# Attention into an expert layer on one core: short score transposes first, an ACT copy in each slot's chain, softmax work on DVE behind that chain

## The chip, the core and the metric

The kernel runs on one core of one Trainium2 chip. The core has a matrix engine (TensorE, PE in the profile; its weight loads are the row PEld), a vector engine (VectorE, DVE), an activation engine (ScalarE, ACT), GpSimd (POOL) and SyncE (SP), which here only issues DMAs. The metric is the device time of one execution in microseconds, as the median of several runs.

## What is computed

Memory attention for 8 batches and 8 heads, 576 positions of 64 numbers, with 32 memory slots, followed by one expert layer (a SiLU between two matrix products) over all 4608 tokens of 512 numbers, with 2048 hidden units. All in float32.

```python
a = softmax(phi, axis=2)                       # phi: 8 x 8 x 576 x 32
k_m = einsum('bhsm,bhsd->bhmd', a, k)          # 32 memory keys a head
v_m = einsum('bhsm,bhsd->bhmd', a, v)
attn = softmax(q @ k_m.T / 8, axis=-1)         # 576 x 32 a head
x = attn @ v_m                                 # to 4608 x 512
h = x @ w_in
out = (h * sigmoid(h)) @ w_out
```

## The kernel before

The product attn @ v_m @ w_in is folded: for each batch, v_m times w_in gives a small matrix `pm` (256 rows for 8 heads of 32 slots, `p_mm`), and the hidden values are `pm` times the attention weights. Each float32 factor is split into a high part, rounded to a shorter format (fp32r), and a low part, the rest; a product is high x high + high x low + low x high. A high part is a copy that rounds, a low part a subtraction.

The eight batches run one after another. Batches 0 and 1 use plain products, batches 2 to 7 a Strassen form of the second product (7 products of sums in place of 8). A batch of the second kind has 16 slots (2 halves t of the tokens, 8 steps j each). In one slot:

- PE computes the hidden values of the slot (`ffn1s`, L807, 12 matmuls into the PSUM tile `h`, of which there is one), then the matmuls of events, then the second product of the slot before (`st_step`, through `product` at L838, 21 matmuls: 14 with high parts, tile `aparts`, then 7 with low parts, tile `gparts`).
- `forms` turns `h` into the factors of the second product: ACT applies SiLU (L818, into `gbuf`; L820 does the leftover tokens, into `gleft`, and with it `h` is read) and rounds three of the blocks (L822). DVE forms four differences (L823, L826, L827), and rounds and subtracts. This is called the slot's chain here.
- Events put the attention of the next batch between the slots. By slot, in batches 2 to 6: 1, 2 and 3 are phi's maximum, its fold over partitions and its subtraction on DVE (L256 to L313); 4 its exponential on ACT (L317); 5 and 7 the products with k and v (`e_mm`, L333); 8 their transposes (`e_tr`, and the copy L366); 9 the scores (`s_all`), which go into PSUM as 512 columns a pair in the tile `bg` and 64 columns a pair in a free part of `h`, and are transposed by DVE from both; 10 the scores' maximum and subtraction on DVE (L424, L428); 11 their exponential on ACT (L432); 12, 13 sum and scaling (L436, L442); 14 transposes back (L453) and the split of the weights (`s_high` L458, `s_low` L463). `p_mm` in slots 1, 3, 13 and 15 is followed by its own split (ACT L644, DVE L646).
- After slots 7 and 15 `st_out` adds up the sums and stores them (ACT L869, seven DVE additions at L874).

What orders the work: PE's instructions stay in the order of the code throughout, ACT's from batch 1 on. DVE's order there is found by the scheduler at build time, within the dependencies; `behind(i, other)` adds a dependency of order between two instructions. ACT's functions lie in tables, so an exponential between SiLUs comes with two table loads (ACT_TABLE_LOAD).

Of the kernel before, what the change touches and what calls it, by code (L numbers as in the profile page):

```python
# [15 lines left out]
AF = mybir.ActivationFunctionType  # L16
ALU = mybir.AluOpType
# [10 lines left out]
JW = 512  # L28
# [20 lines left out]
def attn_ffn_kernel(  # L49
# [9 lines left out]
    nc = tc.nc  # L59
# [60 lines left out]
    raws, cvas, last_silu, last_split = {}, {}, [], []  # L120
# [249 lines left out]
    def s_all(b):  # L370

        sc = at[b]["sc"] = sb.tile([P, 2, S], F32, tag="att", name=f"sc{b}")
        bg, left = bgtile(), beside_h(S - 512)
        kvT = at[b]["kvT"]
        w = 512 - HALF
        for hf, f, n in ((0, 0, HALF), (1, 0, w), (1, w, HALF - w)):
            for r in range(NR):
                for p in range(2):
                    to = left[p] if f else bg[:, p, hf * HALF : hf * HALF + n]
                    nc.tensor.matmul(  # L380
                        to[M * r : M * (r + 1)],
                        kvT[D * p : D * (p + 1), 0, r],
                        at[b]["q", hf][D * p : D * (p + 1), r, f : f + n],
                        start=True, stop=True, skip_group_check=True,
                    )
        for p in range(2):
            nc.vector.transpose(sc[:, p, :512], bg[:, p])
        for p in range(2):
            nc.vector.transpose(sc[:, p, 512:], left[p])  # L389

    def s_mm(b, hf):
        if "sc" not in at[b]:
# [208 lines left out]
    ALL, FIRST, SECOND = (0, S), (0, HALF), (HALF, S)  # L601
# [211 lines left out]
    def forms(b, t, j, h):  # L813


        g = form_src
        w = MAIN // 2
        nc.scalar.activation(gbuf[:, :MAIN].rearrange("p (i f) -> p i f", i=2), h[:, :, :w], AF.Silu)  # L818
        o = b % 2 * LEFT + t * (LEFT // 2)
        nc.scalar.activation(gleft[:, 2 * j : 2 * j + 2, o : o + LEFT // 2], h[:, :, w:HALF], AF.Silu)  # L820
        hi, lo = form_high[j % 2], form_low[j % 2]
        nc.scalar.activation(hi[:, :3], g[:, 1:4], AF.Copy)  # L822
        nc.vector.tensor_tensor(  # L823
            g[:, 4:6], g[:, :1].broadcast_to([P, 2, P]), g[:, 1:3], op=ALU.subtract
        )
        nc.vector.tensor_tensor(g[:, 6], g[:, 1], g[:, 5], op=ALU.subtract)  # L826
        nc.vector.tensor_tensor(g[:, 7], g[:, 3], g[:, 6], op=ALU.subtract)  # L827
        nc.vector.tensor_copy(hi[:, 3:], g[:, 4:])  # L828
        nc.vector.tensor_tensor(lo, g[:, 1:], hi, op=ALU.subtract)  # L829
        return hi, lo  # L830

    def product(bank, place, part, k, w, first):
# [86 lines left out]
    events = {}  # L919

    def ev(b, slot, fn, *a):
        events.setdefault((b, slot), []).append((fn, a))

    for b in range(B):
        n = b + 1
        if b == 0:
            for j in range(2, DFF // CW):
                ev(b, 2 * j - 1.5, p_mm, b, j * CW, CW)
        elif b == 1:
            ev(b, 0, win_save)  # L930
            for j in range(1, NJ):
                ev(b, 4 * j - 3, p_mm, b, j * JW, JW)
            for j in range(NP):
                ev(b, 1.5 * j + 2, w_forms, j, 0)
                ev(b, 1.5 * j + 2.5, w_forms, j, 1)
        else:
            ev(b, 0, win_load, b, 3)
            ev(b, 1, p_mm, b, 2 * JW, JW)
            ev(b, 3, p_mm, b, 3 * JW, JW)
            if b > 2:  # L940
                ev(b, 1, s_high, b, SECOND)
                ev(b, 1, s_low, b, SECOND)
        if n == B:
            continue
        at_slot = (
            (4, 5, 6, 7.5, 9, 9.5, 11.5, 12.5, 13, 13.5, 13.5, 14) if b == 0
            else (1, 2, 3, 5, 9, 10, 10, 11, 12, 13, 13, 14) if b == 1
            else (1, 2, 4, 5, 8, 9, 9, 10, 11, 12, 13, 14)
        )
        mx, sub, ex, em, tr, s0, s1, sx, se, ss, sn, sk = at_slot  # L950
        ev(b, mx, phi_max, n)
        if n == 1:
            ev(b, sub, phi_allmax, n, (0, 1), (0,))
            ev(b, sub + 0.5, phi_allmax, n, (0, 1), (1,))
        else:
            for i in range(3):
                ev(b, sub, phi_fold, n, i)
        ev(b, 3 if b > 1 else sub + 0.5, phi_sub, n)
        ev(b, ex, phi_exp, n)
        if n < 3:  # L960
            ev(b, em, e_mm, n)
            ev(b, 14 if b == 0 else em + 1, load_kv, n + 1, range(FULLC if b == 0 else 2))
        else:
            ev(b, em, e_mm, n, range(2))
            ev(b, em, load_kv, n, range(2, FULLC))
            ev(b, em + 2, e_mm, n, range(2, FULLC))
            if n + 1 < B:
                ev(b, em + 2, load_kv, n + 1, range(2))
        ev(b, tr, e_tr, n)
        ev(b, em, load_q, n, 1)  # L970
        if n == 1:
            ev(b, s0, s_mm, n, 0)
            ev(b, s1, s_mm, n, 1)
        else:
            ev(b, s0, s_all, n)
        if n + 1 < B:
            ev(b, s1, load_q, n + 1, 0)
        ev(b, sx, s_max, n, ALL)
        ev(b, sx, s_sub, n, ALL)
        ev(b, se, s_exp, n, ALL)  # L980
        ev(b, ss, s_sum, n, ALL)
        ev(b, sn, s_norm, n, ALL)
        u = ALL if n < 3 else FIRST
        ev(b, sk, s_back, n, u)
        ev(b, sk, s_low, n, u)
        if n + 1 < B:
            ev(b, sk, load_phi, n + 1)
        if b == 0:
            ev(b, 14, p_mm, n, 0, JW)
        else:  # L990
            for k in range(3):
                ev(b, 6 + k if b == 1 and k < 2 else 10 + 2 * k, win_load, n, k)
            for k in range(2):
                ev(b, (12 if b == 1 else 13) + 2 * k, p_mm, n, k * JW, JW)
# [115 lines left out]
    def behind(i, other):  # L1110
        tc.add_manual_dep(
            i,
            other.ins.name,
            mybir.DependencyInfo(mybir.DependencyClass.NoSync, mybir.DependencyReason.DATA),
            reason="behind",
        )

    def finish(tiles):
        if prev is None:
            return  # L1120
        if prev[0] == "main":
            main_step(prev[1], prev[2], prev[3], tiles)
        elif prev[0] == "left" and tiles[0] == 0:
            if prev[1] < 2:
                left_step(prev[1], prev[2], prev[3])
                t1_load(prev[2])
            else:
                left_st(prev[1], prev[2], prev[3])
        elif prev[0] == "st" and tiles[0] == 0:
            st_step(*prev[1:])  # L1130

    for b in range(B):
        if b == 1:
            whole.close()
            ctx.enter_context(in_order(ACT))
        for s in range(NFC if b > 1 else 0):
            t, j = divmod(s, NP)
            h = ffn1s(b, t, j)
            part = forms(b, t, j, h)
            for part_ in range(2):  # L1140
                for fn, a in events.pop((b, s + part_ / 2), []):
                    fn(*a)
            finish(range(NI))
            prev = ("st", b, t, j, part)
        for fc in range(NFC if b < 2 else 0):
            if b == 0 and fc < 2:
                for part in range(2):
                    for fn, a in events.pop((b, fc + part / 2), []):
                        fn(*a)
                continue  # L1150
            h = ffn1(b, fc)
            gs = split(silu(b, fc, h))
            for part in range(2):
                if b == 0:
                    finish((2 * part, 2 * part + 1))
                traced = nc.cur_bb.bb.instructions
                n = len(traced)
                for fn, a in events.pop((b, fc + part / 2), []):
                    fn(*a)
                if b == 0:  # L1160
                    for i in list(nc.cur_bb.bb.instructions)[n:]:
                        if i.engine == ACT:
                            behind(i, last_silu[-1])
                        elif i.engine == DVE and fc > 10:
                            behind(i, last_split[-1])
            if b:
                finish(range(NI))
            prev = ("main", b, fc, gs)
        if b % 2:
            for n in range(NLS):  # L1170
                gs = left_split(b, n)
                finish((0, 1, 2, 3))
                prev = ("left", b, n, gs)
# [56 lines left out]
```

## Time and profile before

| | us |
|---|---|
| median of 3 runs | 711.97 (710.71 to 712.09) |
| the profiled execution | 712.11 |
| its span | 710.2 |
| PE busy in the span | 682.6 (96%) |
| PE's weight loads busy | 601.2 (85%) |
| DVE busy | 549.4 (77%) |
| ACT busy | 307.6 (43%) |

Busy shares are means over stages with different limits; batches 2 to 7 fill the span from 200.9 us on. A row of the order of time has the start in us from the span's start, the duration in us, engine, line, operation, result<-sources, shape and count, and in brackets the idle time of that engine just before and what ended it. A row of a group has busy time in us, mean duration in ns, then idle time before. A row of waits has who waited for whom: us in total, times, the longest. A row of a stretch has, for each engine, busy us, and then the share of the clock granted to PE.

### The profile page before, as it was taken

What the parts mean: (1) busy time and instruction counts of PE and PEld (TensorE: products, weight loads), DVE (VectorE), ACT (ScalarE), POOL (GpSimd) and SP (SyncE); (2) the same over time, 40 slices, a digit from 0 to 9 for tenths busy, and PEclk for the clock granted to TensorE, in tenths of its full rate; (3) what the DMA queues carried; (4) which work ended last, traced back from release to release, by engine and by line L of the source; (5) the groups of instructions that cost most, each with busy time, mean ns of one, the idle gap of its engine ahead of it and who ended that gap; (6) DMA issues with size and microseconds to landing.
All of it is one profiled execution on the core that took longest, in us unless ns stands there. A gap on an engine that the chain in (4) does not pass through costs nothing.

```text
span 710.2 us, 14595 instructions
## 1 busy us (share of the span) xinstructions
PE 682.6 (96%) x5932; PEld 601.2 (85%) x5932; DVE 549.4 (77%) x1109; ACT 307.6 (43%) x578; POOL 0.7 (0%) x6
## 2 busy tenths in 40 slices
PE   8999999999999989998999989999899998999997
PEld 3578777887889988898988989889889998889996
DVE  4898799788776778968869687887886867886663
ACT  3879674534524344342513424453432433442320
POOL 0000000000000000000000000000000000000000
PEclk9999999999999999999999999999999999999999
DMA  9998966304441344034420254203541024300001
GB/s 344 336 349 254 338 234 220 107 36 156 160 140 59 118 176 152 32 112 179 154 90 16 76 216 152 90 18 122 212 153 45 2 60 149 116 35 1 31 1 45
DMA packets 32946, 93.88 MB, mean 132 GB/s; under 512 B 2928, under 2 KB 13296, under 8 KB 29296
## 3 DMA queue, kind: packets, MB, share of 16 engines
q1 hardware_dynamic: 31936, 90.19, 36.3%
q10 hardware_dynamic: 944, 2.77, 1.0%
q8 instruction: 47, 0.77, 0.4%
q14 instruction: 19, 0.16, 0.1%
HBM read 77.22 MB, written 15.73 MB: 131 GB/s over the span
## 4 chain that ended last, share of the span: by engine, by line
PE 55%; DVE 22%; ACT 5%; issue 3%; DVEq 0%; ACTq 0%
PE sum L838 20%; PE h L807 15%; PE acc L706 6%; PE lsum L838 5%; DVE gparts L829 4%; PE h L665 4%; PE bg L628 2%; DVE oo L874 2%; DVE pm L646 2%; ACT gbuf L818 2%; DVE gbuf L823 2%; PE accleft L706 2%; PE bg L333 1%; DVE aparts L828 1%; DVE aT L453 1%
## 5 line engine op out<-in xcount | busy, mean ns | idle before, releaser
L807 PE MATMUL h<-aparts,pm 128*128 128x288 f32 x1152 | 170.9, 298 | 10.0 <-DVE sc L389 10.0
L818 ACT ACTIVATE gbuf<-h 128x512 f32<-128x512 f32 x96 | 57.4, 598 | 273.2 <-PE h L807 191.3
L807 PEld LDWEIGHTS h<-aparts,pm 128*128 128x128 f32 x1152 | 158.7, 190 | 11.0 <-issue 10.8
L829 DVE TENSOR_TENSOR gparts<-gbuf,aparts 128x896 fp32r<-128x896 f32 x96 | 104.7, 1091 | 8.4
L838 PE MATMUL sum<-wo_hi,aparts 128*128 128x256 f32 x384 | 105.6, 297 | 0.0
L838 PE MATMUL sum<-kept,aparts 128*128 128x256 f32 x576 | 101.2, 284 | 1.5 <-DVE oo L874 1.3
L838 PE MATMUL sum<-wo_lo,aparts 128*128 128x256 f32 x384 | 101.4, 285 | 0.0
L823 DVE TENSOR_TENSOR gbuf<-gbuf 128x256 f32<-128x256 f32 x96 | 40.7, 424 | 78.3 <-ACT gbuf L818 78.0
L838 PEld LDWEIGHTS sum<-wo_hi,aparts 128*128 128x128 f32 x384 | 74.2, 193 | 20.9 <-issue 12.7
L706 PE MATMUL acc<-wo_hi,gparts 128*128 128x512 f32 x256 | 86.4, 396 | 0.2
L838 PEld LDWEIGHTS sum<-kept,aparts 128*128 128x128 f32 x576 | 83.5, 193 | 2.3 <-DVE oo L874 2.3
L838 PEld LDWEIGHTS sum<-wo_lo,aparts 128*128 128x128 f32 x384 | 74.5, 194 | 0.0
L838 PE MATMUL sum<-wo_hi,gparts 128*128 128x256 f32 x384 | 73.8, 284 | 0.5
L838 PE MATMUL sum<-kept,gparts 128*128 128x256 f32 x288 | 65.5, 282 | 0.0
L838 PEld LDWEIGHTS sum<-wo_hi,gparts 128*128 128x128 f32 x384 | 59.3, 190 | 1.8 <-DVE gparts L829 1.5
L706 PEld LDWEIGHTS acc<-wo_hi,gparts 128*128 128x128 f32 x256 | 47.8, 188 | 14.2 <-DVE gparts L682 2.0
L665 PEld LDWEIGHTS h<-aparts,pm 128*128 128x128 f32 x372 | 51.7, 188 | 8.6 <-issue 2.3
L665 PE MATMUL h<-aparts,pm 128*128 128x288 f32 x372 | 56.3, 299 | 1.9 <-DVE aparts L463 1.0
L706 PE MATMUL acc<-wo_lo,gparts 128*128 128x512 f32 x128 | 50.5, 394 | 0.8 <-DVE wo_lo L182 0.8
L822 ACT ACTIVATE aparts<-gbuf 128x384 fp32r<-128x384 f32 x96 | 50.4, 525 | 0.0
L838 PEld LDWEIGHTS sum<-kept,gparts 128*128 128x128 f32 x288 | 47.9, 190 | 0.0
L828 DVE CAST aparts<-gbuf 128x512 fp32r<-128x512 f32 x96 | 40.7, 424 | 8.1 <-DVE phi L313 0.3
(197 smaller groups left out, 927.7 us busy)
## 6 DMA issues: line engine op xcount, KB each, us to landing
win<-win_saved SPq DMA_DIRECT2D x24, 1024.0 KB, 4.8
kv<-in_kv SPq DMA_DIRECT2D x28, 516.0 KB, 4.6
q<-in_q SPq DMA_DIRECT2D x16, 576.0 KB, 6.6
raw<-in_w_in SPq DMA_DIRECT2D x14, 512.0 KB, 7.8
out<-oo SPq DMA_DIRECT2D x27, 256.0 KB, 2.2
raw<-in_w_out SPq DMA_DIRECT2D x6, 1024.0 KB, 6.0
win_saved<-win SPq DMA_DIRECT2D x4, 1024.0 KB, 8.7
phi<-in_phi SPq DMA_DIRECT2D x7, 576.0 KB, 5.6
```

Source lines behind the costliest of these rows:

```text
L628: nc.tensor.matmul(bg[M * r : M * (r + 1), p, :w].rearrange("p (k f) -> p k f", f=P), kvT[D * p : D * (p + 1), 1, r], src[D * p : D * (p + ...
L646: nc.vector.tensor_tensor(lo[:, :, c], bg[:, :, :w], hi[:, :, c], op=ALU.subtract)
L665: nc.tensor.matmul(h[:, hf, :HALF], wt[:, p, fs], a[:, p, hf * HALF : (hf + 1) * HALF], start=n[hf] == 0, stop=n[hf] == 5, skip_group_chec ...
L706: nc.tensor.matmul(acc[key], gt[:, cs], wt[:, fc], start=fc == 0 and n == 0, stop=fc == NFC - 1 and n == 2)
L807: nc.tensor.matmul(h[:, i, :HALF], wt[:, p, f : f + P], a[:, p], start=n == 0, stop=n == 5)
L818: nc.scalar.activation(gbuf[:, :MAIN].rearrange("p (i f) -> p i f", i=2), h[:, :, :w], AF.Silu)
L822: nc.scalar.activation(hi[:, :3], g[:, 1:4], AF.Copy)
L823: nc.vector.tensor_tensor(g[:, 4:6], g[:, :1].broadcast_to([P, 2, P]), g[:, 1:3], op=ALU.subtract)
L828: nc.vector.tensor_copy(hi[:, 3:], g[:, 4:])
L829: nc.vector.tensor_tensor(lo, g[:, 1:], hi, op=ALU.subtract)
L838: nc.tensor.matmul(sums[bank][:, place * Q : (place + 1) * Q], gt[:, k], wt, start=bank not in begun, stop=True, skip_group_check=True,)
L874: nc.vector.tensor_tensor(to, a, c, op=op)
```

## The change

Four edits. In `s_all` the transposes of the two 64-column pieces (in `h`) come ahead of those of the 512-column pieces (in `bg`). In `forms` the rounding of the four differences moves from DVE to ACT (L828 after), and the one subtraction of seven blocks becomes two, of three (L829 after) and of four blocks (L830 after). In the batches from 2 on, every DVE instruction that an event issues, but those of `s_all`, is put behind the last subtraction of its slot's chain. And two events move: the split of the second half of the tokens from slot 1 to slot 6, and `p_mm` of slot 3 to the second half of that slot.

```diff
         for p in range(2):
+            nc.vector.transpose(sc[:, p, 512:], left[p])
+        for p in range(2):
             nc.vector.transpose(sc[:, p, :512], bg[:, p])
-        for p in range(2):
-            nc.vector.transpose(sc[:, p, 512:], left[p])
...
-        nc.vector.tensor_tensor(g[:, 7], g[:, 3], g[:, 6], op=ALU.subtract)
-        nc.vector.tensor_copy(hi[:, 3:], g[:, 4:])
-        nc.vector.tensor_tensor(lo, g[:, 1:], hi, op=ALU.subtract)
+        s4 = nc.vector.tensor_tensor(g[:, 7], g[:, 3], g[:, 6], op=ALU.subtract)
+        nc.scalar.activation(hi[:, 3:], g[:, 4:], AF.Copy)
+        behind(nc.vector.tensor_tensor(lo[:, :3], g[:, 1:4], hi[:, :3], op=ALU.subtract).ins, s4)
+        last_split.append(nc.vector.tensor_tensor(lo[:, 3:], g[:, 4:], hi[:, 3:], op=ALU.subtract))
...
-            ev(b, 3, p_mm, b, 3 * JW, JW)
+            ev(b, 3.5, p_mm, b, 3 * JW, JW)
             if b > 2:
-                ev(b, 1, s_high, b, SECOND)
-                ev(b, 1, s_low, b, SECOND)
+                ev(b, 6, s_high, b, SECOND)
+                ev(b, 6, s_low, b, SECOND)
...
                 for fn, a in events.pop((b, s + half_slot / 2), []):
+                    traced = nc.cur_bb.bb.instructions
+                    n = len(traced)
                     fn(*a)
+                    for i in list(nc.cur_bb.bb.instructions)[n:]:
+                        if i.engine == DVE and fn is not s_all:
+                            behind(i, last_split[-1])
```

Where instructions stand now. First DVE in batch 2 at the scores' transposes, from the end of slot 8's additions to the end of slot 9's chain (`sc` are the scores, `x` and `oo` the additions), before:

```order
L874 TENSOR_TENSOR oo<-x,sum_2121 128x256
L823 TENSOR_TENSOR gbuf<-gbuf 128x256
L826 TENSOR_TENSOR gbuf<-gbuf 128x128
L387 STREAM_TRANSPOSE sc_2573<-bg 128x512
L827 TENSOR_TENSOR gbuf<-gbuf 128x128
L387 STREAM_TRANSPOSE sc_2573<-bg 128x512
L828 CAST aparts<-gbuf 128x512
L389 STREAM_TRANSPOSE sc_2573<-h 128x64
L829 TENSOR_TENSOR gparts<-gbuf,aparts 128x896
L389 STREAM_TRANSPOSE sc_2573<-h 128x64
```

and after:

```order
L823 TENSOR_TENSOR gbuf<-gbuf 128x256
L875 TENSOR_TENSOR oo<-x,oo 128x256
L826 TENSOR_TENSOR gbuf<-gbuf 128x128
L875 TENSOR_TENSOR oo<-oo 128x256
L875 TENSOR_TENSOR oo<-x,oo 128x256
L875 TENSOR_TENSOR oo<-x,sum_2123 128x256
L827 TENSOR_TENSOR gbuf<-gbuf 128x128
L829 TENSOR_TENSOR gparts<-gbuf,aparts 128x384
L387 STREAM_TRANSPOSE sc_2583<-h 128x64 x2
L830 TENSOR_TENSOR gparts<-gbuf,aparts 128x512
L389 STREAM_TRANSPOSE sc_2583<-bg 128x512 x2
```

Both readers of `h` stand ahead of the long transposes now, and behind the first low part of the chain, whose first pieces stand among the additions.

Second ACT in batch 2 at phi's exponential, slot 4, before:

```order
L818 ACTIVATE gbuf<-h 128x512
L820 ACTIVATE gleft<-h 128x2x32
L822 ACTIVATE aparts<-gbuf 128x384
L317 ACT_TABLE_LOAD
L317 ACTIVATE phi_1900<-phi_1900 128x1152
L818 ACT_TABLE_LOAD
```

and after:

```order
L818 ACTIVATE gbuf<-h 128x512
L820 ACTIVATE gleft<-h 128x2x32
L822 ACTIVATE aparts<-gbuf 128x384
L828 ACTIVATE aparts<-gbuf 128x512
L317 ACT_TABLE_LOAD
L317 ACTIVATE phi_1900<-phi_1900 128x1152
L818 ACT_TABLE_LOAD
```

The exponential stands behind the new copy; so does the scores' (L432) in slot 11. On DVE the work that leads to it, before (phi's subtraction, then slot 0's chain, the first of the batch):

```order
L310 TENSOR_TENSOR phi_1900<-phi_1900,am 128x512
L313 TENSOR_TENSOR phi_1900<-phi_1900,am 64x128
L310 TENSOR_TENSOR phi_1900<-phi_1900,am 128x512
L313 TENSOR_TENSOR phi_1900<-phi_1900,am 64x128
L823 TENSOR_TENSOR gbuf<-gbuf 128x256
```

and after (the end of slot 3's chain, phi's subtraction, the low part of `pm`, and slot 4's chain):

```order
L830 TENSOR_TENSOR gparts<-gbuf,aparts 128x512
L310 TENSOR_TENSOR phi_1900<-phi_1900,am 128x512
L313 TENSOR_TENSOR phi_1900<-phi_1900,am 64x128
L310 TENSOR_TENSOR phi_1900<-phi_1900,am 128x512
L313 TENSOR_TENSOR phi_1900<-phi_1900,am 64x128
L646 TENSOR_TENSOR pm<-bg,pm 128x1024
L823 TENSOR_TENSOR gbuf<-gbuf 128x256
L826 TENSOR_TENSOR gbuf<-gbuf 128x128
L827 TENSOR_TENSOR gbuf<-gbuf 128x128
```

Phi's work moved from ahead of slot 0's chain to between slot 1's and slot 4's.

Third DVE in batch 2 from slot 10 to slot 11, before (row maximum and subtraction, then slot 10's chain):

```order
L424 TENSOR_REDUCE smx<-sc_2573 128x36
L428 TENSOR_TENSOR sc_2573<-sc_2573,smx 128x1152
L823 TENSOR_TENSOR gbuf<-gbuf 128x256
L826 TENSOR_TENSOR gbuf<-gbuf 128x128
L827 TENSOR_TENSOR gbuf<-gbuf 128x128
```

and after (the end of slot 10's chain, the two, then slot 11's chain):

```order
L829 TENSOR_TENSOR gparts<-gbuf,aparts 128x384
L830 TENSOR_TENSOR gparts<-gbuf,aparts 128x512
L424 TENSOR_REDUCE smx<-sc_2583 128x36
L428 TENSOR_TENSOR sc_2583<-sc_2583,smx 128x1152
L823 TENSOR_TENSOR gbuf<-gbuf 128x256
L826 TENSOR_TENSOR gbuf<-gbuf 128x128
L827 TENSOR_TENSOR gbuf<-gbuf 128x128
```

Maximum and subtraction moved from ahead of slot 10's chain to ahead of slot 11's.

More of the change, by code (lines that the diff above doesn't have):

```diff
@@ L1139, in attn_ffn_kernel @@
             part = forms(b, t, j, h)
-            for part_ in range(2):
-                for fn, a in events.pop((b, s + part_ / 2), []):
+            for half_slot in range(2):
+                for fn, a in events.pop((b, s + half_slot / 2), []):
+                    traced = nc.cur_bb.bb.instructions
+                    n = len(traced)
                     fn(*a)
+                    for i in list(nc.cur_bb.bb.instructions)[n:]:
+                        if i.engine == DVE and fn is not s_all:
+                            behind(i, last_split[-1])
             finish(range(NI))
```

## The prediction

> **What bounds the kernel now.** I read the page's busy times first, then the waits, then the order of time around each place where TensorE stood still.
>
> ```profile
> PE 682.6 (96%) x5932; PEld 601.2 (85%) x5932; DVE 549.4 (77%) x1109; ACT 307.6 (43%) x578; POOL 0.7 (0%) x6
> ...
> ACT gbuf L818 <- DVE gparts L829: 81.8, 25, 5.2
> ...
> PE h L807 <- DVE sc L389: 10.0, 5, 2.0
> ...
> PEld bg L333 <- ACT phi L317: 2.9, 4, 1.2
> ```
>
> PE is the bound: a slot of a Strassen batch without side work takes 4.11 us (L807 at 256.67 and 260.78, below). What can be won or lost is where PE stands still, and the row of L807 names the largest such place: five times, 2.0 us each, the next slot's hidden product waits for the short score transposes. The row above it says that DVE falls behind in part of each batch, since the silu of a slot had to wait for the slot before. PE's order of time there:
>
> ```profile
> 248.60 0.40 PE L838 MATMUL sum<-kept,gparts 128*128 128x256 f32 x2
> 250.99 2.73 PE L807 MATMUL h<-aparts,pm 128*128 128x288 f32 x12 [1.99 <-DVE sc L389]
> 256.67 1.76 PE L807 MATMUL h<-aparts,pm 128*128 128x288 f32 x12
> 260.78 1.76 PE L807 MATMUL h<-aparts,pm 128*128 128x288 f32 x12
> 264.90 1.36 PE L807 MATMUL h<-aparts,pm 128*128 128x288 f32 x9
> 270.31 1.76 PE L807 MATMUL h<-aparts,pm 128*128 128x288 f32 x12
> 274.78 0.70 PE L807 MATMUL h<-aparts,pm 128*128 128x288 f32 x4
> ...
> 251.00:254.90 3.90, 3.90 (x19) 3.90 (x20) 3.07 (x4) 1.15 (x3) 0.00 (x0) 0.57 0.79 321
> 331.00:334.90 3.90, 3.90 (x31) 3.90 (x32) 3.69 (x6) 1.16 (x3) 0.00 (x0) 1.00 0.84 343
> ```
>
> The row of 248.60 holds two matmuls; in the stream one follows the other after 0.12 (33 in 4.11), so the second starts at 248.72, and 250.99 is 2.15 late. Slot 10 then takes 5.68 (250.99 to 256.67) in place of 4.11, because the granted clock was 0.57 there; after the same wait in batch 3 it was 1.00 and nothing was lost. By the same views batches 4 and 6 go as batch 2, and 5 as 3.
>
> **The change, part by part.** All sums are made against the profiled execution (712.11, span 710.2, so 1.9 around it; the median of the runs is 711.97).
>
> *The slot's chain.* Durations:
>
> ```profile
> L829 DVE TENSOR_TENSOR gparts<-gbuf,aparts 128x896 fp32r<-128x896 f32 x96 | 104.7, 1091 | 8.4
> L828 DVE CAST aparts<-gbuf 128x512 fp32r<-128x512 f32 x96 | 40.7, 424 | 8.1 <-DVE phi L313 0.3
> L682 DVE TENSOR_TENSOR gparts<-gbuf,gparts 128x512 fp32r<-128x512 f32 x32 | 21.9, 686 | 0.3
> L788 ACT ACTIVATE kept<-wf 128x512 fp32r<-128x512 f32 x5 | 3.1, 630 | 4.3 <-DVE wf L774 4.3
> 207.64 0.42 DVE L823 TENSOR_TENSOR gbuf<-gbuf 128x256 f32<-128x256 f32 x1 [1.58 <-ACT gbuf L818]
> 208.43 0.29 DVE L827 TENSOR_TENSOR gbuf<-gbuf 128x128 f32<-128x128 f32 x1
> ...
> L428 DVE TENSOR_TENSOR sc<-sc,smx 128x1152 f32<-128x1152 f32 x7 | 9.5, 1356 | 0.2
> L424 DVE TENSOR_REDUCE smx<-sc 128x36 f32<-128x1152 f32 x7 | 9.5, 1351 | 0.2
> ```
>
> The 512-wide cast (0.42) leaves DVE and becomes an ACT copy of 0.63 (same form, L788). The 896-wide subtract (1.09) becomes 384 and 512 wide: 0.69 by L682, and 0.56 between 0.42 (256 wide) and 0.69. DVE's work falls by 0.26 a slot, 25 us in all, but off PE's path. The second subtract waits for ACT: L827 starts 0.79 after L823 and ends 0.29 later; 0.10 to reach ACT (an estimate: DVE's last transpose reached PE after 0.15, below, and ACT's exponential after 0.06), 0.63, and 0.69: 2.5 us from the chain's start to its end, of which 0.08 overlaps what follows, so 2.44. Before, the next instruction started after 2.72 (207.64 to L646 at 210.36, below). A gain of 0.3 a chain, with a hole in it that nothing now fills. The new price is on ACT's queue: whatever ACT does for a slot's events now stands behind a copy that DVE must first release. ACT's queue is in code order, so the two exponentials (phi in slot 4, scores in slot 11) with their table loads wait for DVE's chain of that slot. Before, they stood behind a copy that needs the silu alone.
>
> *Phi's exponential (slot 4), whose result e_mm (L333, slot 5) waits for.* Batch 2 before:
>
> ```profile
> 222.32 0.42 DVE L823 TENSOR_TENSOR gbuf<-gbuf 128x256 f32<-128x256 f32 x1 [1.36 <-ACT gbuf L818]
> 222.86 1.28 ACT L317 ACT_TABLE_LOAD   x1
> 224.15 1.17 ACT L317 ACTIVATE phi<-phi 128x1152 f32<-128x1152 f32 x1
> 225.69 1.09 PE L333 MATMUL bg<-kv,phi 128*32 128x129 f32 x32
> 195.75 0.69 DVE L256 TENSOR_TENSOR mt<-phi 128x512 f32<-128x512 f32 x1
> 202.77 0.29 DVE L313 TENSOR_TENSOR phi<-phi,am 64x128 f32<-64x128 f32 x1
> 210.36 1.22 DVE L646 TENSOR_TENSOR pm<-bg,pm 128x1024 fp32r<-128x1024 f32 x1
> ...
> 303.08 0.29 DVE L313 TENSOR_TENSOR phi<-phi,am 64x128 f32<-64x128 f32 x1
> 304.49 1.16 ACT L317 ACTIVATE phi<-phi 128x1152 f32<-128x1152 f32 x1
> 305.71 0.54 PE L333 MATMUL bg<-kv,phi 128*32 128x129 f32 x12 [0.65 <-ACT phi L317]
> ```
>
> The exponential ended at 225.32, 0.4 ahead of PE. All of phi's work on DVE was then done between 195.75 and 203.06 (first and last of its 20 instructions), ahead of slot 0's chain; now it stands behind slot 1's. It takes 7.3 there, less 0.7 for an L682 in between and some 0.5 where chain pieces now fill its holes: 6.1. From slot 1's L823 (207.64) DVE runs without a break: three chains at 2.44 (7.3), phi 6.1, pm's low part (L646, 1.14 to the next) twice 2.3: 15.7, so slot 4's L823 starts at 223.4 and not 222.32. From there to PE: 0.79 + 0.29 + 0.10 + 0.63 + 1.29 + 1.17 + 0.06 = 4.3, so L333 starts at 227.7 and PE waits 2.1. Batches 4 and 6 the same (the leftover step ahead of them lets DVE catch up). In batch 3 phi's subtraction ended at 303.37 with DVE busy all along; L463 leaves (0.7), the fillers of the holes leave too, so I take 303.1. Then L646 (1.14) and 4.3: L333 at 308.5, where PE wants it at 305.06 (305.71 less 0.65): 3.4; batch 5 alike. Sum 3 x 2.1 + 2 x 3.4 = 13.1, less what is lost there now (1.7 to 2.9 by PE's and its loads' waits, I take 2.2): +10.9. Bounds: 0, if DVE gets there 2 us earlier, and +15.
>
> *The scores' exponential (slot 11).* Before:
>
> ```profile
> 259.09 0.53 ACT L822 ACTIVATE aparts<-gbuf 128x384 fp32r<-128x384 f32 x1
> 259.64 1.28 ACT L432 ACT_TABLE_LOAD   x1
> ...
> 263.41 0.60 ACT L818 ACTIVATE gbuf<-h 128x512 f32<-128x512 f32 x1
> 263.90 0.22 ACT L820 ACTIVATE gleft<-h 128x64 f32<-128x64 f32 x1
> ```
>
> The silu of slot 12 was late, but h came free at 264.12, 0.8 ahead of L807 at 264.90. Count now from T, the end of slot 10's L807. Chain 10 starts at T+0.7 and ends at T+3.2; row maximum and subtraction (L424, L428) now come behind it: T+5.9; chain 11's L823 only then; its copy on ACT ends at 5.8 + 1.08 + 0.10 + 0.63 = T+7.6; load, exponential, load take 3.77 (259.64 to 263.41): T+11.3; silu and gleft 0.7: T+12.0. PE, which needs 12.3 for three slots and is 1.75 into them at T, asks at T+10.55: it waits 1.5. Five batches: +7.7; bounds 0 (the slack was 0.8) and +12.
>
> *The short transposes first.* Between chain 8's end and the short transposes now stand the kvT copy, the seven adds and most of chain 9:
>
> ```profile
> 243.22 1.09 DVE L829 TENSOR_TENSOR gparts<-gbuf,aparts 128x896 fp32r<-128x896 f32 x1
> 244.22 0.42 DVE L874 TENSOR_TENSOR x<-sum,oo 128x256 f32<-128x256 f32 x1
> 247.00 0.42 DVE L823 TENSOR_TENSOR gbuf<-gbuf 128x256 f32<-128x256 f32 x1
> 250.60 0.24 DVE L389 STREAM_TRANSPOSE sc<-h 128x64 f32<-128x64 f32 x1
> ...
> 165.78 0.50 PE L665 MATMUL h<-aparts,pm 128*128 128x288 f32 x2 [0.59 <-DVE sc L389]
> ```
>
> The adds take 2.8 (244.22 to 247.00), chain 9's pieces between them 0.9, its first low part 0.5, the copy 0.2, the short ones 0.45: from 244.1 to 248.9 where 250.84 stood, about when PE asks. The adds now end near 247.8, and PE's next sum bank asks for the last of them at 247.4: I keep 0.45 lost, of 2.15 (0 to 1.2). Five batches: -8.5; in batch 1 the same edit takes 0.6 (the row at 165.78).
>
> *The rest.* Slot 14 took 4.47 (270.31 to 274.78), 0.36 over, as its sums waited for a late chain; with softmax work behind the chain that goes: -1.8. High and low part of the second half move from slot 1 to slot 6, two slots ahead of their use; each is half as wide as L428, so under 1.36, and slot 6 has no other event: hidden, and if not, 1.4 a batch. pm's half slot moves nothing past a queue. No DMA moves, on SP's queue or POOL's.
>
> *The clock.* The three slowed stretches (5.68 less 4.11 each) go with their waits: -4.7. The new waits at L333 are as long or longer. A wait of 2.15 was followed by half clock 3 times in 5; I take 2.5 of 5 now: +3.9.
> By the Trainium skill (TensorE: Matmul & The Clock Gate, HAM oscillation — how this bites in real kernels) it takes PE-idle gaps of over some 3.4 us to throttle. The rows above differ, with 0.57 after 2.15, and decide; by that rule the +3.9 falls away, and the sum is 715.1: rival (b).
>
> **The sum.** +10.9 + 7.7 - 8.5 - 0.6 - 1.8 - 4.7 + 3.9 = +6.9: 719.0.
>
> **Rivals.** (a) Faster: e_mm's wait does not grow, because DVE, 25 us lighter, reaches slot 4's chain 2 us earlier than I count. Then -10.9 and no new half clock, -3.9: 704.2. The point: with e_mm waiting under about 1.6 us on average (2.6 counted), and half clock in proportion, the change breaks even. For it: 81.8 us of silu waits on L829 may shrink. Against: phi's work is put later by order, and the exponential behind one chain more. (b) The clock stays full at all new waits, since their idle time falls between two of the spans by which it is granted, as in batch 3 (1.00 after the same wait): -3.9, 715.1; against it the 0.57 in batch 2. (c) The clock drops after every e_mm wait and some of slot 11's: +4 to +8: 725. (d) h comes free no sooner, as the adds and the chain now stand ahead of the short transposes: +8.5 and the old half clocks kept: 732; against it the count above, 2 us to spare.
>
> **How the numbers follow.** Forecast 0.44, (b) 0.15, (c) 0.11, (d) 0.02; (a) 0.22; a part of (a) that ends near no change 0.06. 0.2% (1.4 us) is about what a measurement can tell from no change. Slower 0.72, same 0.06, faster 0.22. Own range of the forecast 713 to 725; to leave out no more than 2 in 10 it reaches into (a) and (c): 703 to 727.
>
> **What would show it.** Waits of PE on L389 gone or under 1 us; PE waiting for L317 five times, 2 to 3.5 us; ACT's table loads L317 and L432 starting right behind an L828 copy, 2 us later against PE than before; L807 of slot 13 waiting for gleft by 1.5; half clock after e_mm. Wrong would be: L333 starting with PE's stream, or the exponentials ending ahead of it; then (a).

## The result, and the profile after

The median after is 718.64 us (4 runs, 717.77 to 719.41), beside 712.03 (4 runs) of the kernel before: a ratio of 1.0096 (95% interval 1.0076 to 1.0116). The change makes the kernel slower by 0.96%. The profiled execution took 719.41, with a span of 717.6: 7.4 us more than the span before. The four times lie in pairs near 717.8 and 719.4, at granted clocks of 0.992 and 0.989 over the whole run, a difference of about one stretch of 3.4 us at half clock (0.0024 of 717.6), which costs 1.5 us (below).

The page's busy times after:

```profile
span 717.6 us, 14742 instructions
...
PE 684.0 (95%) x5932; PEld 601.9 (84%) x5932; DVE 516.8 (72%) x1109; ACT 367.1 (51%) x674; POOL 0.7 (0%) x6
```

DVE lost 32.6 us of work, ACT got 59.5 more, and PE, the bound, was idle for 33.6 us in place of 27.6. The waits after, who for whom:

```profile
PEld bg L333 <- ACT phi L317: 13.4, 5, 3.4
PE bg L333 <- ACT phi L317: 12.2, 5, 3.2
...
PE h L807 <- ACT gleft L820: 6.4, 5, 1.3
...
PE sum L839 <- DVE oo L875: 2.2, 6, 0.7
```

The row of L807 on the score transposes (10.0 before) is gone. Two new rows are there, both of them waits for ACT, and one small one for the additions. The costliest groups, for the split copy and the low parts:

```profile
L828 ACT ACTIVATE aparts<-gbuf 128x512 fp32r<-128x512 f32 x96 | 60.7, 633 | 100.2 <-DVE gbuf L827 100.2
...
L830 DVE TENSOR_TENSOR gparts<-gbuf,aparts 128x512 fp32r<-128x512 f32 x96 | 66.5, 693 | 20.5 <-ACT aparts L828 20.5
...
L829 DVE TENSOR_TENSOR gparts<-gbuf,aparts 128x384 fp32r<-128x384 f32 x96 | 52.9, 551 | 0.1
```

The first row is the price of the change: ACT stood in front of the copy for about a microsecond a slot, on the average of 96 (100.2 in all), held by DVE's difference, and whatever came next in ACT's queue stood with it. The order of time around slot 4 of batch 2 shows what that was, first DVE, then ACT, then PE:

```profile
222.81 0.41 DVE L823 TENSOR_TENSOR gbuf<-gbuf 128x256 f32<-128x256 f32 x1
...
223.59 0.29 DVE L827 TENSOR_TENSOR gbuf<-gbuf 128x128 f32<-128x128 f32 x1
```

```profile
223.91 0.63 ACT L828 ACTIVATE aparts<-gbuf 128x512 fp32r<-128x512 f32 x1 [1.73 <-DVE gbuf L827]
224.56 1.28 ACT L317 ACT_TABLE_LOAD   x1
225.86 1.16 ACT L317 ACTIVATE phi<-phi 128x1152 f32<-128x1152 f32 x1
```

```profile
223.35 1.75 PE L807 MATMUL h<-aparts,pm 128*128 128x288 f32 x12
227.07 1.09 PE L333 MATMUL bg<-kv,phi 128*32 128x129 f32 x32 [1.97 <-ACT phi L317]
228.09 0.58 PE L839 MATMUL sum<-wo_hi,aparts 128*128 128x256 f32 x1
```

ACT was idle for 1.73 and then had copy, load and exponential to do one after the other. PE stood still from 225.10 to 227.07, and the matmul behind took 0.58 where its like took 0.28. The same in slot 11, whose exponential delays the silu of slot 12 and with it slot 13's L807:

```profile
261.37 0.63 ACT L828 ACTIVATE aparts<-gbuf 128x512 fp32r<-128x512 f32 x1 [1.54 <-DVE gbuf L827]
262.02 1.28 ACT L432 ACT_TABLE_LOAD   x1
263.32 1.17 ACT L432 ACTIVATE sc<-sc 128x1152 f32<-128x1152 f32 x1
264.50 1.28 ACT L818 ACT_TABLE_LOAD   x1
265.80 0.60 ACT L818 ACTIVATE gbuf<-h 128x512 f32<-128x512 f32 x1
266.29 0.22 ACT L820 ACTIVATE gleft<-h 128x64 f32<-128x64 f32 x1
```

```profile
264.87 0.40 PE L839 MATMUL sum<-kept,gparts 128*128 128x256 f32 x2
266.56 1.73 PE L807 MATMUL h<-aparts,pm 128*128 128x288 f32 x11 [1.30 <-ACT gleft L820]
```

The part that was to help did help. In slot 9 of batch 2 (DVE, then PE) the short transposes ended at 252.29, 0.5 ahead of slot 10's L807, which followed its stream:

```profile
250.91 0.41 DVE L875 TENSOR_TENSOR oo<-x,sum 128x256 f32<-128x256 f32 x1
251.25 0.28 DVE L827 TENSOR_TENSOR gbuf<-gbuf 128x128 f32<-128x128 f32 x1
251.45 0.55 DVE L829 TENSOR_TENSOR gparts<-gbuf,aparts 128x384 fp32r<-128x384 f32 x1
251.92 0.37 DVE L387 STREAM_TRANSPOSE sc<-h 128x64 f32<-128x64 f32 x2
```

```profile
251.38 0.75 PE L839 MATMUL sum<-kept,aparts 128*128 128x256 f32 x4 [0.30 <-DVE oo L875]
...
252.79 0.42 PE L807 MATMUL h<-aparts,pm 128*128 128x288 f32 x2
```

What was late there now is the last addition (250.91 to 251.32), which a sum bank waits for.

### The profile page after: what moved, and what is told of

Read it like the earlier page. It is cut to its first block, busy times and chain, and to the rows that moved or that the text cites. A ratio compares the mean times of both kernels' runs of the same rounds, so it can differ in the third digit from the quotient of the medians.

```text
span 717.6 us, 14742 instructions
## 1 busy us (share of the span) xinstructions
PE 684.0 (95%) x5932; PEld 601.9 (84%) x5932; DVE 516.8 (72%) x1109; ACT 367.1 (51%) x674; POOL 0.7 (0%) x6
## 4 chain that ended last, share of the span: by engine, by line
PE 52%; DVE 20%; ACT 10%; issue 4%; DVEq 0%; ACTq 0%
PE sum L839 18%; PE h L807 12%; PE acc L706 7%; PE lsum L839 5%; PE h L665 4%; ACT aparts L828 3%; DVE gbuf L823 2%; PE bg L628 2%; DVE pm L646 2%; DVE oo L875 2%; DVE gbuf L826 2%; DVE gbuf L827 2%; PE bg L333 2%; ACT gbuf L818 2%; DVE gparts L830 2%
## 5 line engine op out<-in xcount | busy, mean ns | idle before, releaser
L807 PE MATMUL h<-aparts,pm 128*128 128x288 f32 x1152 | 169.0, 296 | 6.4 <-ACT gleft L820 6.4
L807 PEld LDWEIGHTS h<-aparts,pm 128*128 128x128 f32 x1152 | 157.0, 188 | 7.6 <-ACT gleft L820 7.4
L823 DVE TENSOR_TENSOR gbuf<-gbuf 128x256 f32<-128x256 f32 x96 | 40.5, 422 | 114.4 <-ACT gbuf L818 113.9
L828 ACT ACTIVATE aparts<-gbuf 128x512 fp32r<-128x512 f32 x96 | 60.7, 633 | 100.2 <-DVE gbuf L827 100.2
L830 DVE TENSOR_TENSOR gparts<-gbuf,aparts 128x512 fp32r<-128x512 f32 x96 | 66.5, 693 | 20.5 <-ACT aparts L828 20.5
L829 DVE TENSOR_TENSOR gparts<-gbuf,aparts 128x384 fp32r<-128x384 f32 x96 | 52.9, 551 | 0.1
```

Of the source, the lines that this page charges most:

```text
L807: nc.tensor.matmul(h[:, i, :HALF], wt[:, p, f : f + P], a[:, p], start=n == 0, stop=n == 5)
L823: nc.vector.tensor_tensor(g[:, 4:6], g[:, :1].broadcast_to([P, 2, P]), g[:, 1:3], op=ALU.subtract)
L828: nc.scalar.activation(hi[:, 3:], g[:, 4:], AF.Copy)
L829: behind(nc.vector.tensor_tensor(lo[:, :3], g[:, 1:4], hi[:, :3], op=ALU.subtract).ins, s4)
L830: last_split.append(nc.vector.tensor_tensor(lo[:, 3:], g[:, 4:], hi[:, 3:], op=ALU.subtract))
```

## Where the time went, slot by slot

A slot's length is the distance from its first L807 to the next slot's. Summed over batches 2 to 7, against the fastest kernel found (the cast on DVE in slots 4 and 11, and DVE's order behind the chain in slots 1 to 7 alone; experiment 9), in us. Slots left out differ by less than 0.05.

| kernel | slot 1 | 5 | 9 | 10 | 12 | 13 | 14 | 15 | all |
|---|---|---|---|---|---|---|---|---|---|
| before | 1.0 | 2.2 | 9.3 | 4.5 | 0 | 0.6 | 1.8 | 1.5 | 21.0 |
| after | 0 | 18.7 | 2.2 | -0.4 | 7.2 | 0.6 | 0 | 0.8 | 29.0 |
| 1: cast on DVE in all slots | 1.0 | 0 | 6.7 | 0 | 0 | 0 | 0 | 2.0 | 9.7 |
| 2: cast on DVE in slots 4, 11 | 0 | 0 | 2.2 | -0.4 | 0 | 0 | 0 | 0 | 1.8 |
| 3: without the order behind the chain | 0 | 10.5 | 0 | 0 | 2.5 | 0.5 | 0 | 0 | 13.5 |
| 4: before, short transposes first | 1.0 | 2.1 | 1.0 | 0 | 2.2 | 4.2 | 1.8 | 1.5 | 13.9 |
| 5: after, PE kept busy ahead of L333 | 0 | 12.6 | 2.2 | -0.4 | 7.2 | 0.6 | 0 | 0.8 | 22.9 |
| 8: cast on DVE in slot 4 | 0 | 0 | 2.1 | -0.4 | 7.2 | 0.6 | 0 | 0.8 | 10.3 |

The first two rows hold the result: slot 5 lost 16.5, slot 12 7.2, and slots 9 and 10 gave back 12.1. Outside these batches the kernel after is 0.7 us shorter (batch 2 begins at 200.22 in place of 200.88, batch 1's gain).

## Experiments

The theory: the copy on ACT holds up the two exponentials that come behind it in ACT's queue, and PE waits for both; the rest of the change gains time. The rivals: the copy is harmless and the order of DVE behind the chain, which puts phi's and the scores' work late, is what costs; or the clock has nothing to do with PE's waits. Each ratio is to the kernel before run beside that experiment (710.7 to 710.8 us).

**1. The copy back on DVE, everything else kept.**

```diff
-        nc.scalar.activation(hi[:, 3:], g[:, 4:], AF.Copy)
+        nc.vector.tensor_copy(hi[:, 3:], g[:, 4:])
```

> The changed kernel, with the 512-wide rounding of each slot back on DVE in all slots; the two low parts, the order behind the chain and the moved events stay. Theory A (the copy on ACT is what makes the exponentials late, since it puts them behind DVE's chain of their own slot): PE's wait for phi's exponential at e_mm falls from 12.2 us in all to 3 or less, the wait for gleft ahead of slot 13 from 6.4 to under 1, half clock after e_mm goes, 700 us (696 to 706). Rival B (the softmax work behind the chain on DVE makes the exponentials' inputs late by itself): both waits stay over two thirds of their size, 713 to 719.

Measured: 700.23 us, ratio 0.9857 (0.9837 to 0.9877). The theory's number, and the rival falls: with the order of DVE kept and only the copy back, both waits for ACT are gone, and so is every stretch at half clock but the one at the kernel's end. What PE waits for of DVE instead:

```profile
PEld sum L839 <- DVE oo L875: 4.6, 9, 1.3
...
PE sum L839 <- DVE oo L875: 2.6, 6, 1.1
PE h L807 <- DVE sc L387: 2.1, 5, 0.4
```

**2. The copy on DVE only in the slots of the exponentials.**

```diff
-        nc.scalar.activation(hi[:, 3:], g[:, 4:], AF.Copy)
+        if 8 * t + j in (4, 11):
+            nc.vector.tensor_copy(hi[:, 3:], g[:, 4:])
+        else:
+            nc.scalar.activation(hi[:, 3:], g[:, 4:], AF.Copy)
```

> The changed kernel, with the rounding back on DVE in slots 4 and 11 alone, the two slots whose events hold an exponential. Theory A: the same waits go as with all slots back, 700 us (695 to 706), and if DVE's lighter load helps elsewhere it is faster than with all slots back. Rival B: 715 to 719.

Measured: 692.29 us, ratio 0.9742 (0.972 to 0.9764); PE is now busy for 98% of the span:

```profile
PE 675.5 (98%) x5932; PEld 595.9 (86%) x5932; DVE 521.3 (75%) x1121; ACT 359.4 (52%) x662; POOL 0.7 (0%) x6
```

Below every time expected, and 7.9 us below experiment 1. So the copy on ACT in the other 14 slots is worth 7.9 us: 4.5 in slot 9, 2.0 in slot 15, 1.0 in slot 1 (table). My expectation here took over from the prediction that DVE's lighter work is off PE's path; that was wrong.

**3. Without the order behind the chain, the copy on ACT kept.** The loop that calls `behind` for the events' instructions is left out.

```diff
-                        if i.engine == DVE and fn is not s_all:
-                            behind(i, last_split[-1])
+                        pass
```

> The changed kernel without the order that puts the events' DVE work behind the slot's chain; the copy stays on ACT, the short transposes first. Phi's work is then ahead of slot 0's chain in batch 2 again. Theory A: the exponentials still stand behind the copy, but its chain is no longer late; e_mm waits about 1 in batches 2, 4, 6 and 2 in 3, 5, 7 us in all, gleft 1 to 2 in all: 706 us (702 to 711). Rival B (order alone): e_mm waits 2 us in all as before the change, 699 to 702. If neither, and the copy costs all of it: 716 or more.

Measured: 703.87 us, ratio 0.9893 (0.9863 to 0.9923), as expected. The waits:

```profile
PE bg L333 <- ACT phi L317: 7.1, 5, 2.3
PE h L807 <- ACT gleft L820: 1.7, 5, 0.3
```

12.2 and 6.4 after have become 7.1 and 1.7. The copy ahead of the exponential makes these waits, and the order, which puts DVE's softmax work late, makes them longer: taking away the copy removes both (experiment 1, where the order stays), taking away the order, worth some 15 us here, only part of them. Without the copy the order makes no wait for the exponentials at all.

**4. The kernel before with the short transposes first, and nothing else.**

```diff
+        for p in range(2):
+            nc.vector.transpose(sc[:, p, 512:], left[p])
         for p in range(2):
             nc.vector.transpose(sc[:, p, :512], bg[:, p])
-        for p in range(2):
-            nc.vector.transpose(sc[:, p, 512:], left[p])
```

> The kernel before, with nothing but the short transposes issued first. The scheduler puts them behind one long transpose and one chain piece. By the working of the prediction h comes free 1.5 us sooner, PE's wait on the transposes falls from 10.0 us to 3 or so, half clock in slot 10 goes: 712 less 7.5, 4.7 and 0.6 = 699 us (697 to 704). Rival: what is won is lost again in slots 11 to 13, as DVE falls behind there: 706 to 712.

Measured: 704.42 us, ratio 0.9916 (0.9895 to 0.9936), between theory and rival. Slots 9 and 10 give 12.9 us (table), but 2.2 come back in slot 12 and 3.6 in slot 13, where now

```profile
PEld h L807 <- ACT gleft L820: 2.4, 5, 0.5
PE h L807 <- DVE sc L387: 1.6, 5, 0.3
...
PE h L807 <- ACT gleft L820: 1.4, 5, 0.3
```

In batch 2 PE reaches slot 12 3.6 us earlier than before (257.18, 260.78), while DVE, which has as much to do as before, starts the last subtraction of that slot's chain only 2.4 us earlier (265.79, 268.23). A wait removed ahead of a loaded engine is partly found again behind it.

**5. The changed kernel with PE kept busy in the waits at L333.** The products go to `bg`, which L333 overwrites. (Lines from there on stand two further down: L335 is L333, L809 is L807.)

```diff
+        if b > 2 and cs[0] == 0:
+            keep_warm(pt[0], 9 if b % 2 else 14)
         turns = [(c, p) for c in cs for p in range(2)]
```

> The changed kernel with idle-filling matmuls on PE ahead of e_mm in batches 3 to 6 (14 or 9 bf16 matmuls of 512 columns, whose results are overwritten), about as long as PE waits there, so that the wait for ACT stays but PE isn't idle in it. Theory A: the half-clock stretches behind the waits of e_mm come from PE's idle time in them. Then three of the four go (batch 2 keeps its own), about 1.55 us each, and the time is 714.0 (712.5 to 715.5). Rival B: the idle time isn't what lowers the clock; the stretches stay and the time is 718.6 (717.5 to 720).

Measured: 713.22 us (6 runs, 713.03 to 713.51), ratio 1.0035 (1.0022 to 1.0047): 5.4 below the changed kernel. The edit's `b` is the batch whose attention is computed, so slot 5 of batch 2 got its filling as well, and all four stretches are gone, not three as I expected. The exponential comes no earlier:

```profile
223.41 1.75 PE L809 MATMUL h<-aparts,pm 128*128 128x288 f32 x12
225.00 2.12 PE L80 MATMUL bg<-ident 128*128 128x512 bf16 x9
227.13 1.09 PE L335 MATMUL bg<-kv,phi 128*32 128x129 f32 x32
```

L335 starts 3.72 after the slot's first matmul, as L333 did (223.35 to 227.07), and the slot takes 7.34 in place of 8.86. PE's idle time lowers the clock, and that costs 1.5 us each time.

**6. Experiment 2 with the moved events back in their old places.**

```diff
-            ev(b, 3.5, p_mm, b, 3 * JW, JW)
+            ev(b, 3, p_mm, b, 3 * JW, JW)
             if b > 2:
-                ev(b, 6, s_high, b, SECOND)
-                ev(b, 6, s_low, b, SECOND)
+                ev(b, 1, s_high, b, SECOND)
+                ev(b, 1, s_low, b, SECOND)
```

> The kernel with the cast on DVE in slots 4 and 11 alone (692.3 us), and the two moved events back where they were (high and low part of the second half in slot 1, p_mm of slot 3 in its first half). Theory A: slot 1 of batches 3, 5 and 7, which got 0.34 us shorter by the change, gets longer again, and nothing else moves: 693.3 (692.5 to 694.5). Rival B: DVE's late work in slot 1 pushes phi's subtraction and so the exponential of slot 4 back by 1 to 2 us, and PE waits again at L333: 696 to 700. Rival C: no difference, 692.3 (691.5 to 692.5).

Measured: 693.04 us (692.94 to 693.34), 0.7 above experiment 2. The size is theory A's, its place isn't: slot 1 stays as short, and the 0.6 us are lost in slot 5. Slot 1's gain came with the copy on ACT, as experiment 1 shows too (1.0 in slot 1, with the events moved).

**7. Experiment 2 without the order behind the chain** (the edit of experiment 3).

> The kernel with the cast on DVE in slots 4 and 11 alone (692.3 us), without the order of DVE behind each slot's chain. Theory A: the order behind the chain is worth something once the exponentials don't wait for it: without it the chains of slots 9 to 14 run late as in the kernel with the short transposes alone (slot 13 0.8 us, slot 14 0.36 us, slot 12 0.4 us longer, in five or six batches): 697 to 701. Rival B: DVE is lighter by the copies on ACT, the scheduler's order is good enough, and without the order it is as fast or faster: 690 to 693.

Measured: 691.55 us (691.42 to 691.91), ratio 0.973 (0.9717 to 0.9743): rival B. Slot 9 gets 2.2 shorter, slot 10 0.4 and slot 5 1.0 longer. Once DVE is lighter, the order behind the chain is worth nothing as a whole; how it makes slot 9 longer is shown under the short transposes below.

**8. The copy on DVE in slot 4 alone,** to price the two waits apart.

```diff
-        if 8 * t + j in (4, 11):
+        if 8 * t + j in (4,):
```

> The changed kernel with the cast back on DVE in slot 4 alone; in slot 11 the scores' exponential still stands behind the copy on ACT. This prices the two waits apart. Theory A: the wait at L333 goes (12.2 us, and the four half-clock stretches with it, 6 us), the one at slot 13 for gleft stays (5 x 1.45): 699.8 (698 to 701.5). Rival B: slot 13's wait is itself a result of the late slot 4, and goes too: 692 to 694.

Measured: 700.68 us (700.49 to 700.75), ratio 0.9857 (0.9844 to 0.9871): theory A. L333's wait of 12.2 has gone, slot 13's stands as it was after:

```profile
PE h L807 <- ACT gleft L820: 6.4, 5, 1.3
```

So the copy in slot 4 costs 18.0 us (718.64 less 700.68; 18.7 by slot 5 of the table, of which 12.6 stay without the clock, in experiment 5), the one in slot 11 8.4 (700.68 less 692.29; by the table in slots 12, 13 and 15).

**9. The order behind the chain in slots 1 to 7 alone,** on top of experiment 2.

```diff
-                        if i.engine == DVE and fn is not s_all:
+                        if i.engine == DVE and fn is not s_all and s < 8:
```

> The kernel with the cast on DVE in slots 4 and 11 alone, with DVE's order behind the chain only in slots 1 to 7 (phi's work), none from slot 8 on. With that order everywhere it took 692.3 us, without it anywhere 691.6. Theory A: the order costs 0.4 us in slot 9 (short transposes and additions) and gains 0.2 us a batch in slot 5, so this takes the better of both: 690.6 (690.0 to 691.2). Rival B: slot 9 goes by where slots 0 to 7 leave DVE, not by the order there: 692.3 (691.8 to 692.8).

Measured: 690.46 us (690.37 to 690.73), ratio 0.9708 (0.969 to 0.9725): theory A, and the fastest kernel found, 2.9% faster than before. Its remaining waits in these slots are

```profile
PE h L807 <- DVE sc L387: 1.2, 5, 0.2
...
PE sum L842 <- DVE oo L878: 0.7, 1, 0.7
```

**10. Experiment 9 with the long transposes first again** (the edit of experiment 4 the other way round).

> As the kernel with that order in slots 1 to 7 alone, but with the long transposes ahead of the short ones again, as before the change. This prices the short ones' place by itself, in the faster kernel. Theory A: slot 10's L807 waits for the short transposes again, 1.5 to 2.1 us a batch, and about three of the five waits are followed by half clock (1.5 us): 9 to 14 us above the other kernel of this call, 700 to 705. Rival B: with DVE lighter by the casts that ACT does, the waits stay under 1 us and the clock full: 2 to 5 us above it, 692.5 to 696.

Measured: 697.24 us (697.04 to 697.41), 6.8 above experiment 9, between theory A and rival B: PE waits 1.4 us a batch, near what the theory has, but the clock stays full as the rival has it.

```profile
PEld h L807 <- issue: 8.1, 5, 1.6
PE h L807 <- DVE sc L389: 7.2, 5, 1.4
```

The place of the short transposes is thus worth 6.8 us by itself where the clock doesn't come into it: by the traces 6.0 in slot 9 and 0.9 ahead of batch 2.

## Why the prediction was right, point by point

The forecast was 719.0, and +6.9 on the profiled span; measured are 718.64 and +7.4. Term by term (measured from the table; what experiment 5 leaves in slot 5 is the wait, the rest the clock):

| term | predicted | measured |
|---|---|---|
| wait at L333, slot 5 | +10.9 | +10.4 (12.6 less 2.2) |
| wait for gleft, slot 13's L807 | +7.7 | +7.2 |
| short transposes, slot 9 | -8.5 | -7.1 |
| the same in batch 1 | -0.6 | -0.7 |
| slot 14 | -1.8 | -1.8 |
| old half clock, slot 10 | -4.7 | -5.0 (0.4 of it not the clock) |
| new half clock, slot 5 | +3.9 | +6.2 |
| slots 1, 13 and 15 | none | -1.8 |
| sum | +6.9 | +7.4 |

*Phi's exponential: right, step by step.* I put slot 4's L823 at 223.4; it came at 222.81, and PE's own stream was earlier by the same 0.6 (batch 1's gain). From L823 to L333 I counted 4.3; it was 4.26 (222.81 to 227.07). The predicted wait of 2.1 (2.0 by its own figures, 227.7 less 225.69) was 1.97 by the row above and 1.98 in batches 4 and 6; the 3.4 of batches 3 and 5 was 3.16. Experiments 1 and 8 show the cause: without the copy ahead of the exponential the wait is gone.

*The scores' exponential: right.* By the count from T (slot 10's L807 ends at 254.55) the copy was to end at T+7.6 and gleft at T+12.0; they ended at T+7.45 and T+11.96. The wait was 1.45 (264.99 plus a step of 0.12 to 266.56), predicted 1.5.

*The short transposes: right in kind, the size off by 1.4.* I kept 0.45 of each 2.15 as lost, with the adds as the reason; 0.8 stayed, in the wait for the last addition (0.30 idle by its row, 0.46 to the next step) and the start of the leftover scores (0.26). Batch 7's slot 9, of which nothing was said, got 0.6 shorter. I had the last addition end at 247.8, 4.4 behind slot 9's first L807 (243.41 before); it ended 5.0 behind it (251.32, 246.31 after). What I put at nothing there is ACT's queue once more. The copy L366 on DVE belongs to an event, so it now stands behind slot 8's chain; ACT's L367 waits for it, and ACT's copies of the sums (L869 before, L870 after), which the additions need, stand behind L367. Before, then after:

```profile
242.00 0.25 ACT L367 COPY kvT<-bg 128x128 f32<-128x128 f32 x1
243.02 1.09 ACT L869 ACTIVATE oo<-sum 128x512 f32<-128x512 f32 x2 [0.77 <-PE sum L838]
```

```profile
247.17 0.27 ACT L367 COPY kvT<-bg 128x128 f32<-128x128 f32 x1 [0.96 <-DVE kvT L366]
247.60 1.08 ACT L870 ACTIVATE oo<-sum 128x512 f32<-128x512 f32 x2 [0.17 <-issue]
...
248.24 0.42 DVE L875 TENSOR_TENSOR x<-sum,oo 128x256 f32<-128x256 f32 x1 [1.10 <-ACT oo L870]
```

These copies began 0.39 ahead of slot 9's first L807 before, and 1.29 behind it after. Leaving the order out from slot 8 on gives slot 9 2.2 us (experiment 9 beside experiment 2); that L366 is the instruction that matters is read from these rows, and moving it alone wasn't tried. Slot 9's gain can't be shared out among the edits, since each changes what the others are worth: of its 9.3 us the transposes' place alone leaves 1.0 (experiment 4), the transposes and the order together leave 6.7 (experiment 1), and the copy on ACT brings that to 2.2 (experiment 2).

*The step that failed* is the clause that DVE's work falls "25 us in all, but off PE's path". Its size was right: the cast and the subtractions took 145.4 us before (40.7 and 104.7) and 119.4 after (66.5 and 52.9), 26.0 less; the 32.6 of the page is busy time, in which instructions that overlap count once. But it isn't off PE's path: having the copy on ACT in the other 14 slots is worth 7.9 us of PE's time (experiments 1 and 2). The sum held in spite of it, since most of these 7.9 stood in the sum under slot 9, where my count up to the short transposes leaves the cast out, and the rest (slots 1 and 15) came as a gain that I had not counted.

*The clock: mis-sized.* I took 2.5 of 5 waits to be followed by half clock; it was 4 of 5, 6.2 us in place of 3.9, and experiment 5 takes them away with the wait left in place. Most of this missing 2.3 was made good by the uncounted gains. The nearness of the sum is in part luck: the misses are +1.4 and +2.3 on one side, -1.8, -0.5, -0.5, -0.3 and -0.1 on the other.

*The rivals.* (a) falls: L317's waits grew. (b) falls, with four half-clock stretches; (c) is half right, with four waits of L333 but none of slot 13. (d) falls, `h` was free in time. That the change could have been 2.9% faster, with two slots left out of one of its edits, wasn't among my cases.

## What to carry to other kernels

Before a copy moves to an engine that has time, look at what stands behind it in that engine's queue: an instruction that waits for another engine makes everything behind it wait too, and here the two exponentials, in two of 16 slots, turned a gain of 18.5 us (710.8 to 692.3, run beside each other) into a loss of 6.6 (712.0 to 718.6). Decide such a move slot by slot, not for the loop as a whole. An order on one engine reaches into another's queue as well: DVE's L366, put behind a chain, held up ACT's copies of the sums in slot 9. And a wait taken from the bound engine is only won if the engine behind it has time: the short transposes alone lost 5.8 of their 12.9 us in slots 12 and 13.

## What was not expected of the clock

A stretch at half clock is 3.413 us long every time, but for the one at each kernel's end, and in the three kernels that have several (before, after and experiment 3) all of them start on one grid of that step. In the other nine the grid is laid by the start of the one at the end. With the grid laid over each trace, what decides is PE's idle time inside one step. Over these twelve traces, the first 20 us and the end of each left out, every step with 1.97 us or more of idle time (9 of them: 3 before, 4 after, 2 in experiment 3) was followed by half clock, and no step with 1.44 or less was. None lay between. A row has the stretch, then busy time of PE, PEld, DVE, ACT and POOL, then the clock; after, at L333 in batches 2 and 6:

```profile
224.66:228.07 3.41, 1.44 (x36) 1.02 (x34) 0.61 (x1) 3.38 (x3) 0.00 (x0) 1.00 0.00 0
228.07:231.48 3.41, 3.41 (x20) 3.39 (x17) 2.17 (x5) 2.03 (x5) 0.00 (x0) 0.50 0.78 229
572.81:576.22 3.41, 2.01 (x16) 1.77 (x14) 1.88 (x5) 2.56 (x3) 0.00 (x0) 1.00 0.00 0
576.22:579.63 3.41, 2.84 (x47) 2.64 (x48) 0.88 (x3) 2.96 (x5) 0.00 (x0) 1.00 0.31 65
```

and experiment 10 at slot 10's L807 in batch 2:

```profile
248.29:251.70 3.41, 1.98 (x16) 1.80 (x16) 3.38 (x8) 0.63 (x1) 0.00 (x0) 1.00 0.97 331
251.70:255.11 3.41, 3.41 (x30) 3.41 (x30) 3.08 (x7) 1.79 (x4) 0.00 (x0) 1.00 0.91 368
```

PE was busy for 1.44 of the step ahead of 228.07 and fell to 0.50 for the next; in batch 6 the same wait fell across two steps (1.40 idle in the first), and the clock stayed at 1.00. Before, the wait of batch 3 fell across two steps too (1.08 and 0.91 idle), those of batches 2, 4 and 6 into one (1.99). That is why before showed it in three batches of five, and why rival (b)'s mechanism is real although its outcome wasn't. The Trainium skill (TensorE: Matmul & The Clock Gate, Part 1: The HAM clock gate) has a window of 3413 ns that runs freely, which agrees with the 3.413 here; its table asks for at least one idle window before the clock falls, and here 1.97 us of idle time out of 3.41 were enough, with 1.44 too little. Where between the two the limit lies stays open.
